# One gated-recurrence-and-mixer kernel: rows of 112 become rows of 96, two summands meet on TensorE, signs come from bits, and a new written-out order

## The chip, the cores and the metric

The kernel runs on one core of one Trainium2 chip. The metric is device microseconds from start to end of one execution. Before the change the median of 3 runs is 630.09 us (629.67 to 630.41). The profile is that of one execution. The engines are named as the profile names them: PE is TensorE's matrix multiplication and PEld its loading of weights, DVE is VectorE, ACT is ScalarE, POOL is GpSimd, and SP is SyncE, which issues most of the transfers.

## The reference

Two blocks follow each other. The first is a linear recurrence with a complex gate, for 4 batches, 8 heads, 768 steps and 48 elements a head:

```
mag = sqrt(a_re^2 + a_im^2);  scale = min(mag, 0.999) / (mag + 1e-6)
for t:  S = (a_re + i a_im)[t] * scale[t] * S + k[t] v[t]^T      (the imaginary part of k v^T is 0)
        y[t] = q[t] . Re S
```

The second is a mixer over the joined heads (384 columns). It mixes the steps with a product of rank 32, and then applies two layers with 1,536 hidden columns:

```
u = x + ((x^T U) V)^T
out = u + max(u W1, 0) W2
```

## The kernel before, in words

**Tiling.** A chunk is 128 steps of one batch with all heads, so there are 24 chunks, six to a batch. Two chunks are a group (12 groups). The mixer works on two chunks at a time (12 mixers, numbered 0 to 11), and a batch's three mixers can start only when its six chunks have run, since the rank-32 product sums over all steps. The tables of the weights arrive as 64-bit numbers and are turned into 32-bit ones on DVE and ACT in 13 pieces (`single`), all of it in the first 150 us.

**The gates of a group** (`magnitudes_of`, `within`, `of_blocks`, `turns_of`, `angles`). From `a_re` and `a_im` ACT and DVE form two things: the logarithm of the clipped magnitude, held in `l` after a second summand `y` has been added to it, and the angle, held in `z`. PE then multiplies the logarithms by constant matrices: `mid` gives tile `es ps`, `fore` gives tile `ef ps`, and `total` gives tile `tot`. ACT takes exponentials of these. The angles go through the matrix `prefix` into `ph`. The sign of `a_re` is needed in the angle. For groups 0 to 2 (`BITS`) DVE takes it from the sign bit; from group 3 on ACT computes it with Sign, and one ACT Identity later scales and shifts the angle. From group 3 on (`SPLIT`) the operands of these products are two fp32r parts each (`GS`): ACT (`MADE`) or DVE makes the first part and DVE the remainder.

**A chunk** (`prep`, `chain`). `q` and `k` are multiplied by the exponentials, then by cosine and sine into `QKC`. There a head holds 64 columns of real parts (48 used, 16 zeros) and after them 48 of imaginary parts, so that 112 columns of a head become 112 partitions when PE transposes it (tile `tr`, L860). ACT copies the result into `QK`. Products within the chunk follow (`inner` at L910 and L907, `corners`), DVE scales `QK` in between, a masked copy goes to `DG` and by DMA to `AT`, and `dk` and `y` are the products for the state and the output (L996, L1027, L1035).

**The mixer** (`mixer`). `rank` sums over a batch, `mixed` spreads it, `uTp` transposes, `up` (L1122) is the first layer, and `down` (L1313 for mixer 0, L1356 for the others) is the second. Mixer 0 starts its first layer before batch 0's rank product is known. It is put right afterwards (`put_right`): `rT` (L1136), `rw ps` (L1145), and six `fix` tiles (L1161), which are added to the hidden columns before `down` may use them.

**What sets the order.** Every operation is recorded with its engine. The table `ORDER` gives each one its place in one common row, numbered from 0 to 2670, and each engine executes its own operations in that order. `SPARE` says ahead of which places PE gets filler products of the identity with itself, in blocks of 128 columns, up to three blocks to a product (L1519). A filler is written into a PSUM tile that is free at that place, and is left out where none is free. PE, ACT, DVE, POOL and SP thus each wait in order: an instruction that waits holds up all that stand behind it on its engine.

The two lines that cut the widths, and the call that issues a filler:

```
    DP = 64
    DQ = DP + D
...
        nc.tensor.matmul(out=to[:, 0:k * 128].rearrange("p (k m) -> p k m", k=k), lhsT=ident,
                         rhs=ident.unsqueeze(1).to_broadcast([128, k, 128]), start=True, stop=True)
```

Of the kernel before, what the change touches and what calls it, by code (L numbers as in the profile page):

```python
# [39 lines left out]
        ("POOL", "load"): {0: [14], 1: [34], 1.5: [84], 2: [31]},  # L40
        ("DVE", "load"): {1: [58]},
# [6 lines left out]
        ("ACT", "gates"): {0: [1, 2, 4, 6, 7, 16, 17, 22, 23, 29, 28, 45, 70, 71], 1: [24, 27, 38, 39, 41, 42, 46, 47, 65, 64, 67, 68], 2: [129, 108,  # L48
# [10 lines left out]
        ("DVE", "gates"): {0: [5, 8, 13, 18, 19, 54, 49], 1: [30, 21, 40, 43, 44, 51, 50], 2: [111, 143, 156, 185, 169], 4: [277, 322, 323, 372, 356],  # L59
# [109 lines left out]
        ("POOL", "small"): {0: [932, 933], 1: [1119, 1116, 1117], 2: [1337, 1278, 1338], 3: [1670, 1446, 1515], 4: [1778, 1776, 1777], 5: [2049, 1855,  # L169
        2008], 6: [2154, 2101, 2162], 7: [2343, 2276, 2342], 8: [2633, 2632, 2648], 9: [2629, 2634, 2663], 10: [2635, 2627, 2636]},  # L170
        ("POOL", "angles"): {6: [615], 8: [708, 733], 10: [882, 931], 12: [1097], 14: [1273, 1302], 16: [1472, 1516], 18: [1669], 20: [1879, 1913],
        22: [2039, 2077]},
        ("DVE", "mixing"): {7: [2018, 2019, 2021, 2030, 2032, 2024, 2040, 2102, 2108, 2115, 2120, 2125, 2027]},
}

# [1413 lines left out]
```

## Time and profile before

| what | before |
|---|---|
| median of 3 runs | 630.09 us |
| span of the profiled execution, first to last instruction | 627.0 us |
| PE busy in it | 609.9 us (97%) |
| DVE busy | 499.7 us (80%) |
| ACT busy | 415.8 us (66%) |
| POOL busy | 38.1 us (6%) |
| moved by DMA | 45.74 MB, mean 73 GB/s |

The span is that of one execution and lies 3.1 us under the median of the timed runs. Busy time of PE counts every product, the fillers too. The page cuts the span in 40 slices of 15.7 us and gives busy tenths of each engine. A table by windows gives the same for stretches of one's own choice, with the clock that TensorE was granted. A row of the timeline gives a start, a duration, the engine, the line, the tiles and the number of merged records; in brackets stands the idle time before it and what ended it. Most fp32 products show as two records, a transpose as one.

### The profile page before, as it was taken

How to read it: one execution, taken by the hardware profiler on the slowest of the kernel's cores; microseconds unless marked ns; L12 is line 12 of the kernel's file. 1: busy time of each engine (PE TensorE's matmuls, PEld its weight loads, DVE VectorE, ACT ScalarE, POOL GpSimd, SP SyncE). 2: the span in 40 equal slices, each digit the busy share in tenths (PEclk: the TensorE clock that was granted, in tenths of full speed). 3: DMA queues.
4: the chain of work that ended last, by engine and by line, in shares of the span. 5: the costliest groups of instructions: out<-in, count | busy, mean ns of one | idle time of the engine just before them, and what ended most of it. 6: DMA issues, size and time to landing. Idle time of an engine off the chain costs nothing.

```text
span 627.0 us, 23447 instructions
## 1 busy us (share of the span) xinstructions
PE 609.9 (97%) x10380; PEld 526.2 (84%) x10380; DVE 499.7 (80%) x887; ACT 415.8 (66%) x807; POOL 38.1 (6%) x79
## 2 busy tenths in 40 slices
PE   6998989999999999999999999999999999999998
PEld 3566767666889889889989989888999998999997
DVE  6899999888999979758977867788989884464554
ACT  6999999999898988687787867688433431202010
POOL 5000000000001010010000100000100100000100
PEclk7999999999999999999999999999999999999999
DMA  8864565644143252541512512601203020000101
GB/s 211 191 146 115 135 136 132 155 111 104 33 80 76 50 120 44 99 89 28 99 37 46 113 40 46 124 19 25 63 21 60 9 51 3 1 1 1 45 14 44
DMA packets 173685, 45.74 MB, mean 73 GB/s; under 512 B 167632, under 2 KB 170384, under 8 KB 173584
## 3 DMA queue, kind: packets, MB, share of 16 engines
q1 hardware_dynamic: 171376, 39.90, 30.1%
q0 software_dynamic: 2208, 4.35, 2.1%
q8 instruction: 81, 1.33, 0.9%
q14 instruction: 20, 0.16, 0.1%
HBM read 33.59 MB, written 4.72 MB: 61 GB/s over the span
## 4 chain that ended last, share of the span: by engine, by line
PE 77%; ACT 4%; DVE 3%; DMA 1%; issue 1%; SPq 0%; ACTq 0%; DVEq 0%
PE down L1356 24%; PE up L1122 15%; PE few L1222 11%; PE dk L996 3%; PE tr L860 3%; PE y L1035 3%; PE inner L910 2%; PE down L1313 2%; PE inner L907 2%; PE tot L741 2%; PE y L1027 2%; PE mixed L1089 2%; PE es ps L692 1%; PE ef ps L692 1%; PE uTp L1107 1%; PE corners L971 1%
## 5 line engine op out<-in xcount | busy, mean ns | idle before, releaser
L1122 PE MATMUL up<-uT,w 128*128 128x256 f32 x504 | 116.9, 383 | 0.0
L387 DVE TENSOR_TENSOR QK<-QK,T 112x512 f32<-112x512 f32 (+2 forms) x144 | 102.1, 732 | 8.4 <-PE inner L910 4.3
L1122 PEld LDWEIGHTS up<-uT,w 128*128 128x128 f32 x504 | 93.6, 190 | 12.5
L1356 PE MATMUL down<-w,h 128*128 128x192 f32 x396 | 72.2, 331 | 0.0
L384 ACT ACTIVATE gate<-gate 128x768 f32<-128x768 f32 (+1 forms) x82 | 64.8, 795 | 7.4 <-DVE GS L791 3.2
L1356 PEld LDWEIGHTS down<-w,h 128*128 128x128 f32 x396 | 64.1, 190 | 1.5 <-issue 0.7
L871 ACT COPY QK<-tr 112x512 f32<-112x512 f32 x96 | 51.2, 590 | 14.6 <-PE tr L860 14.3
L390 DVE TENSOR_TENSOR xo<-down,xo 128x192 f32<-128x192 f32 (+1 forms) x79 | 29.9, 387 | 27.5 <-PE down L1356 27.0
L387 DVE TENSOR_TENSOR QKC<-qk,cs 128x768 f32<-128x768 f32 x44 | 41.7, 955 | 6.3 <-ACT cs L384 3.6
L1230 ACT COPY h<-few 128x512 f32<-128x512 f32 x30 | 17.2, 586 | 40.8 <-PE few L1222 40.8
L1356 PE MATMUL down<-stage 128*128 128x192 f32 x198 | 37.6, 331 | 0.0
L1111 ACT COPY uT<-uTp 128x384 f32<-128x384 f32 x22 | 10.0, 479 | 41.4 <-PE uTp L1107 26.9
L1222 PE MATMUL few<-gate,w 128*128 128x128 f32 x280 | 34.8, 275 | 0.0
L1298 POOL DMA_DIRECT2D out_dram<-xo x32 | 19.2, 644 | 243.3 <-DVE xo L390 140.0
L860 PEld LDWEIGHTS tr<-ident,QKC 64*112 64x112 f32 x768 | 24.5, 130 | 10.7 <-issue 4.7
L1222 PEld LDWEIGHTS few<-gate,w 128*128 128x128 f32 x280 | 33.3, 192 | 0.0
L1356 PEld LDWEIGHTS down<-stage 128*128 128x128 f32 x198 | 32.1, 190 | 0.7 <-issue 0.2
L779 POOL DMA_DIRECT2D gate<-F x15 | 12.0, 799 | 327.9 <-DVE w L578 113.5
L860 PE MATMUL tr<-ident,QKC 64*112 64x64 f32 x768 | 29.4, 221 | 2.3 <-DVE QKC L387 1.6
L381 ACT ACT_TABLE_LOAD x24 | 30.8, 1283 | 1.1 <-PEq L1573 0.7
L384 ACT ACTIVATE h<-up 128x512 f32<-128x512 f32 x42 | 24.6, 596 | 9.8 <-PE up L1122 9.5
L976 ACT COPY AT<-corners 32x128 f32<-32x128 f32 x96 | 24.2, 255 | 9.6 <-PE corners L971 8.3
(200 smaller groups left out, 1285.4 us busy)
## 6 DMA issues: line engine op xcount, KB each, us to landing
stage<-in_moe_w_ch_dram SPq DMA_DIRECT2D x12, 768.0 KB, 5.0
qk<-in_q_dram SPq DMA_DIRECT2D x24, 192.0 KB, 3.2
qk<-in_k_dram SPq DMA_DIRECT2D x24, 192.0 KB, 2.7
VP<-in_v_dram SPq DMA_DIRECT2D x24, 192.0 KB, 3.6
gate<-in_a_re_dram SPq DMA_DIRECT2D x22, 192.0 KB, 3.4
gate<-in_a_im_dram SPq DMA_DIRECT2D x22, 192.0 KB, 3.4
AT<-DG SPq DMA_DIRECT2D x96, 32.0 KB, 2.3
T<-E SPq DMA_DIRECT2D x48, 48.0 KB, 2.9
```

The costliest lines, as they stand in the source:

```text
L381: ACT(1.37, rank, lambda: nc.scalar.preload_act_table_set(name), writes=[TABLE])
L384: return nc.scalar.activation(out=o, in_=i, func=f, **kw)
L387: nc.vector.tensor_tensor(out=o, in0=a, in1=b, op=OP.mult)
L390: nc.vector.tensor_tensor(out=o, in0=a, in1=b, op=OP.add)
L860: nc.tensor.transpose(out=get(*ps[r])[0:DQ, h], in_=get(*qkc)[at, h].rearrange("p u d -> p (u d)")[:, 0:DQ], identity=ident[at, at], tile_ ...
L871: nc.scalar.copy(out=to, in_=a)
L976: ACT(0.36, RR, lambda r=r, u=u: nc.scalar.copy(out=get(*ATi).rearrange("p (a u) t -> p a u t", u=2)[r:r + BLK, :, u, BLK:2 * BLK], in_=ge ...
L996: nc.tensor.matmul(out=get(*dk[r])[x:end, h], lhsT=get(*ks)[at, h, x // DP, 0:end - x], rhs=get(*VPi)[at, h], start=True, stop=True, tile_ ...
L1122: nc.tensor.matmul(out=get(*ps)[:, e], lhsT=w1[:, f, (ff + e) * 128:(ff + e + 1) * 128], rhs=get(*uT)[:, f], start=(f == 0), stop=(f == KD ...
L1222: nc.tensor.matmul(out=get(*ps)[:, q], lhsT=w()[:, q * 128:(q + 1) * 128], rhs=v[0](), start=(n == 0 and q == 0), stop=True, skip_group_ch ...
L1298: queue.dma_start(out=out[b, c * CH:(c + 1) * CH, lo:hi], in_=get("xo", i)[:, lo:hi])
L1356: nc.tensor.matmul(out=get(*to)[:, part], lhsT=x(j), rhs=y[:, j], start=(first and j == 0), stop=(j == KH - 1), skip_group_check=not first)
```

## The change

1. The imaginary parts follow the real parts of a head at column 48 instead of 64: `DQ` is 96 instead of 112. `QKC` loses its zero columns between the parts, its multiplications write 768 columns in a row, and the transposes have 96 columns. The two products for the state still write partitions 0 to 63 and 64 to 111, the last 16 of them from the next head's columns, and only 96 are read. The 112 partitions of the tables `T` become 96, and the three memsets of `T` go.
2. In group 0 alone (`SUMMED`) DVE no longer adds `y` to `l`. Each product of the logarithms is done twice instead, once with `y` and once with `l`, accumulated in PSUM.
3. The sign of `a_re` comes from its bits on DVE in all groups. The ACT Sign of groups 3 to 11 goes, and so does their ACT Identity. The shift by a quarter moves into the two operations that make the fp32r parts.
4. `ORDER` and `SPARE` are replaced: another order on every engine and the transfer queues, 2,660 places instead of 2,671, and fillers at other places. 91 filler blocks are issued before (its table asks for 153, and the rest find no free tile) and 89 after, all that its table asks for. After, 24 of them stand ahead of the very first product of the program, where before there were 8.

The diff, cut:

```
-    DQ = DP + D
+    DQ = 2 * D
...
+    SUMMED = (0,)
...
-        QKC.append(singles.tile([128, H, 2, DP], FP, name="QKC%d" % n))
-        nc.gpsimd.memset(QKC[n][:, :, :, D:DP], 0.0)
+        QKC.append(singles.tile([128, H * DQ + DP - (DQ - DP)], FP, name="QKC%d" % n))
+        nc.gpsimd.memset(QKC[n][:, H * DQ:], 0.0)
...
         TS.append(singles.tile([DQ, GC, H * NTOT], FP, name="T%d" % n))
-        nc.gpsimd.memset(TS[n], 1.0)
...
-            if on_dve:
+            if g in SUMMED or g in SPREAD:
                 DVE(c_one(W), R1, lambda: nc.vector.tensor_scalar(out=t(l), in0=t(l), scalar1=-0.5, scalar2=-LNMAX, op0=OP.mult,
                                                                   op1=OP.max), [], [L])
-                DVE(cd, R1, lambda: add(t(l), t(l), t(y)), Y, [L])
+                if g not in SUMMED:
+                    DVE(cd, R1, lambda: add(t(l), t(l), t(y)), Y, [L])
...
-            if g in BITS:
-                DVE(c_one(W), R1, lambda: nc.vector.tensor_scalar(out=t(n).bitcast(U32), in0=t(ar).bitcast(U32), scalar1=0x80000000,
-                                                                  scalar2=INV_PI, op0=OP.bitwise_and, op1=OP.bitwise_or), AR, [N])
-            else:
-                ACT(ca + 0.09, R1, lambda: act(t(n), t(ar), AF.Sign, bias=tiny), AR, [N])
+            DVE(c_one(W), R1, lambda: nc.vector.tensor_scalar(out=t(n).bitcast(U32), in0=t(ar).bitcast(U32), scalar1=0x80000000,
+                                                              scalar2=INV_PI, op0=OP.bitwise_and, op1=OP.bitwise_or), AR, [N])
...
-                    PE(0.65, R1, lambda: nc.tensor.matmul(out=get(*to), lhsT=m.bitcast(FP), rhs=of(l, i), start=True, stop=True),
-                       [L, name], [to, ("sums", g, i)], takes=[keeps], steps=2)
+                    def each():
+                        for u, a in enumerate(parts):
+                            nc.tensor.matmul(out=get(*to), lhsT=m.bitcast(FP), rhs=of(a, i), start=(u == 0), stop=(u == len(parts) - 1))
...
-            if g not in BITS:
-                ACT(ca + 0.09, R2, lambda: act(t(z), t(z), AF.Identity, scale=1.0 / math.pi, bias=fourth), [], Z)
...
-                    ACT(c_act(DM), R2, lambda: nc.scalar.copy(out=of(a, i), in_=of(z, i)), [zi], [a + (i,)])
+                    ACT(c_act(DM) + 0.09, R2, lambda: act(of(a, i), of(z, i), AF.Identity, bias=fourth), [zi], [a + (i,)])
...
-                DVE(c_dve(DM), R2, lambda: nc.vector.tensor_tensor(out=of(b, i), in0=of(z, i), in1=of(a, i).bitcast(FP), op=OP.subtract),
-                    [zi, a + (i,)], [b + (i,)])
+                DVE(c_dve(DM), R2, lambda: nc.vector.scalar_tensor_tensor(out=of(b, i), in0=of(z, i), scalar=0.25, in1=of(a, i).bitcast(FP),
+                                                                          op0=OP.add, op1=OP.subtract), [zi, a + (i,)], [b + (i,)])
```

The two tables of `SPARE`, which read "place: filler blocks ahead of it":

```
-SPARE = {20: 8, 32: 9, 62: 1, 66: 1, 73: 1, 82: 5, 91: 1, 113: 6, 116: 1, 119: 8, 140: 8, 153: 6, 157: 4, 167: 1, 168: 1, 207: 6, 216: 1, 217: 1, 282:
-         1, 352: 2, 436: 1, 514: 5, 518: 5, 527: 4, 546: 4, 547: 25, 551: 12, 596: 2, 601: 1, 606: 3, 624: 1, 632: 3, 646: 1, 653: 1, 664: 1, 672: 2,
-         678: 5, 694: 1, 695: 1, 717: 1, 718: 2}
+SPARE = {28: 24, 79: 6, 86: 2, 100: 9, 118: 4, 143: 9, 151: 3, 158: 2, 193: 2, 217: 3, 237: 1, 257: 5, 262: 2, 270: 4, 287: 1, 294: 4, 301: 1, 311: 1,
+         519: 3, 587: 1, 606: 2}
```

More of the change, by code (lines that the diff above doesn't have):

```diff
@@ L30 @@
 ORDER = {
[9 rows of a table removed]
-        ("POOL", "load"): {0: [14], 1: [34], 1.5: [84], 2: [31]},
-        ("DVE", "load"): {1: [58]},
[6 rows of a table removed]
-        ("ACT", "gates"): {0: [1, 2, 4, 6, 7, 16, 17, 22, 23, 29, 28, 45, 70, 71], 1: [24, 27, 38, 39, 41, 42, 46, 47, 65, 64, 67, 68], 2: [129, 108,
[10 rows of a table removed]
-        ("DVE", "gates"): {0: [5, 8, 13, 18, 19, 54, 49], 1: [30, 21, 40, 43, 44, 51, 50], 2: [111, 143, 156, 185, 169], 4: [277, 322, 323, 372, 356],
[10 rows of a table removed]
-        ("ACT", "angles"): {0: [72, 86, 98, 100, 103], 1: [76, 106, 112, 114, 126], 2: [210, 231, 251, 240, 241, 242, 263, 269, 271], 4: [375, 395,
[5 rows of a table removed]
@@ L172 @@
[L172 to L178 removed]
[9 rows of a table added]
+        ('POOL', 'load'): {0: [11], 1: [62], 1.5: [586], 2: [34]},
@@ new lines @@
+        ('DVE', 'load'): {1: [29]},
[6 rows of a table added]
+        ('ACT', 'gates'): {0: [0, 3, 5, 12, 17, 13, 19, 39, 45, 33, 32, 41, 66, 67], 1: [9, 15, 23, 26, 25, 27, 43, 54, 53, 51, 60, 64], 2: [123, 61,
[10 rows of a table added]
+        ('DVE', 'gates'): {0: [6, 2, 21, 18, 68, 49], 1: [16, 8, 36, 30, 58, 46], 2: [94, 147, 154, 205, 210], 4: [265, 290, 303, 344, 299], 6: [401,
[10 rows of a table added]
+        ('ACT', 'angles'): {0: [71, 85, 91, 92, 98], 1: [80, 95, 107, 116, 112], 2: [211, 225, 239, 238, 232, 243, 251, 250, 256], 4: [369, 385, 413,
[5 rows of a table added]
+        ('DVE', 'angles'): {0: [74, 88], 1: [82, 96], 2: [216, 231, 241], 4: [377, 394, 417], 6: [567, 573, 577, 589, 616, 618, 631], 8: [703, 721,
[4 rows of a table added]
@@ new lines @@
+        ('DVE', 'prep'): {0: [78, 99, 101], 1: [110, 117, 128], 2: [223, 246, 253], 3: [236, 258, 310], 4: [348, 418, 419], 5: [402, 441, 491], 6:
[6 rows of a table added]
+        ('ACT', 'prep'): {0: [120, 115, 121, 119], 1: [137, 159, 160, 161], 2: [260, 277, 274, 272], 3: [291, 305, 328, 335], 4: [434, 439, 440, 438],
[4 rows of a table added]
+        ('DVE', 'rest'): {0: [111, 153, 155, 170, 146, 157, 173], 1: [175, 213, 219, 234, 222, 249, 255, 263], 2: [278, 318, 331, 379, 292, 334, 365,
[8 rows of a table added]
+        ('DVE', 'levels'): {0: [122, 133, 142, 132, 134, 150], 1: [164, 182, 188, 177, 186, 229], 2: [289, 295, 297, 296, 298, 314], 3: [337, 350,
[9 rows of a table added]
@@ new lines @@
+        ('ACT', 'levels'): {0: [140], 1: [201], 2: [304], 3: [393], 4: [477], 5: [538], 6: [747], 7: [808], 8: [942], 9: [1023], 10: [1169], 11:
[14 rows of a table added]
+        ('ACT', 'rest'): {0: [192, 184, 178, 190, 228, 230, 214], 1: [245, 252, 244, 254, 288, 283, 285], 2: [357, 362, 376, 370, 400, 399, 410], 3:
[10 rows of a table added]
+        ('ACT', 'small'): {0: [605, 307, 375, 447, 381, 523, 534, 611, 620, 626], 1: [738, 777, 798, 796, 809, 822, 769], 2: [882, 916, 1081, 1103,
[4 rows of a table added]
+        ('DVE', 'small'): {0: [316, 607, 635, 641, 642, 656, 664, 676, 643, 646, 754, 725], 1: [712, 729, 713, 830, 813, 821, 851, 900, 893, 904, 905,
[25 rows of a table added]
@@ L301 @@
     PL = H * HC
-    BITS = range(SPLIT[0])
     PUT = (0, 2), (4, 6), (8, 10)
@@ L734, in sums @@
                         h, w = at + (u * HH + p) * D, 64 if u == 0 else D
-                        nc.tensor.matmul(out=get(*ps)[u * 64:u * 64 + w, p], lhsT=get(*l)[:, h:h + w], rhs=total, start=True,
-                                         stop=True, tile_position=(0, u * 64))
+                        for n, a in enumerate(parts):
+                            nc.tensor.matmul(out=get(*ps)[u * 64:u * 64 + w, p], lhsT=get(*a)[:, h:h + w], rhs=total, start=(n == 0),
+                                             stop=(n == len(parts) - 1), tile_position=(0, u * 64))
             def at_once():
@@ L744, in of_blocks @@
             else:
-                PE(0.51, R1, sums, [l, ("total", 0), ("sums", g)], [ps], way=1, takes=[e], steps=4 * HH)
+                PE(0.2 + 0.31 * len(parts), R1, sums, [l, ("total", 0), ("sums", g)] + [y + (i,)] * (g in SUMMED), [ps], way=1, takes=[e],
+                   steps=4 * HH * len(parts))
             used = 2 * D if g in SPLIT else 64 + D
@@ L994, in state @@
                     at = slice(r * HC, (r + 1) * HC)
-                    for x, end in ((0, DP), (DP, DQ)):
-                        nc.tensor.matmul(out=get(*dk[r])[x:end, h], lhsT=get(*ks)[at, h, x // DP, 0:end - x], rhs=get(*VPi)[at, h],
+                    for x, w in ((0, DP), (DP, D)):
+                        nc.tensor.matmul(out=get(*dk[r])[x:x + w, h], lhsT=get(*ks)[at, h * DQ + x:h * DQ + x + w], rhs=get(*VPi)[at, h],
                                          start=True, stop=True, tile_position=(r * HC, x))
```

41 lines of the change are left out of this document (19 added, 22 removed), and 248 rows, old and new, of the table ORDER.

## The prediction

> **What bounds the kernel now.** I read the page first: busy times, then the slices.
>
> ```profile
> PE 609.9 (97%) x10380; PEld 526.2 (84%) x10380; DVE 499.7 (80%) x887; ACT 415.8 (66%) x807; POOL 38.1 (6%) x79
> ...
> PE   6998989999999999999999999999999999999998
> ```
>
> PE is busy throughout, but part of that is filler. So I asked for windows, first of everything, then of the filler line L1519 alone (columns: window, length, then busy us of PE, PEld and the rest).
>
> ```profile
> 0.00:30.00 30.00, 23.25 (x118) 13.62 (x118) 23.08 (x50) 22.91 (x45) 8.41 (x32) 0.89 0.84 203
> 30.00:62.00 32.00, 30.07 (x819) 21.50 (x820) 31.66 (x52) 31.07 (x60) 0.00 (x0) 1.00 0.58 134
> 62.00:98.00 36.00, 32.30 (x860) 24.59 (x856) 35.10 (x56) 35.27 (x67) 0.00 (x0) 1.00 0.54 126
> 98.00:126.00 28.00, 27.61 (x491) 19.88 (x487) 25.86 (x42) 26.03 (x51) 0.96 (x1) 1.00 0.61 150
> 126.00:157.00 31.00, 30.08 (x290) 19.76 (x290) 27.34 (x39) 28.45 (x46) 1.53 (x2) 1.00 0.47 109
> 157.00:627.00 470.00, 466.58 (x7830) 426.82 (x7822) 356.66 (x653) 272.12 (x542) 27.16 (x44) 1.00 0.24 49
> ```
>
> ```profile
> 0.00:30.00 30.00, 14.16 (x36) 8.30 (x36) 0.89 0.84 203
> 30.00:62.00 32.00, 8.65 (x30) 4.83 (x28) 1.00 0.58 134
> 62.00:98.00 36.00, 1.08 (x4) 0.68 (x4) 1.00 0.54 126
> 98.00:126.00 28.00, 2.59 (x8) 1.19 (x8) 1.00 0.61 150
> 126.00:157.00 31.00, 4.12 (x16) 2.71 (x16) 1.00 0.47 109
> 157.00:627.00 470.00, 0.00 (x0) 0.00 (x0) 1.00 0.24 49
> sum 627.00, PE 30.61 PEld 17.70; mean PE 5.10 PEld 2.95
> ```
>
> Two stages are to be seen. After 157 us PE runs no filler and is idle for 470.0 - 466.6 = 3.4 us, nearly all of it behind the last product: this stage lasts as long as its products. Before 157 us DVE and ACT are the full engines (66.76 and 66.34 of 68 us from 30 to 98), and PE lacks operands: it is idle for 157.0 - 143.3 = 13.7 us and turns filler for 30.6. I call both together lost time: 44.3 us to 157, 47.7 in all, beside 579.3 us of the kernel's own products. The span is own products plus lost time, and I forecast the two separately. The span of 627.0 lies 3.1 us under the median of 630.09; I carry this difference over.
>
> **The milestone.** The rows that I use from the timeline (start, duration, engine, line, records):
>
> ```profile
> 1.42 3.58 PE L1519 MATMUL tr<-ident 128*128 128x384 f32 x6 [1.42 <-POOL ident masks.py:199]
> 8.79 1.62 PE L696 MATMUL es ps<-GL,mid 128*128 128x384 f32 x2 [3.79 <-DVE GL L390]
> 10.21 4.05 PE L1519 MATMUL tr<-ident 128*128 128x384 f32 x6
> ...
> 16.00 0.81 PE L696 MATMUL ef ps<-GL,fore 128*128 128x384 f32 x2
> ...
> 107.22 0.70 PE L907 MATMUL inner<-QK 112*16 112x16 f32 x64
> ...
> 125.99 1.16 PE L1161 MATMUL fix<-V,rw 32*128 32x256 f32 x16
> ...
> 157.01 5.45 PE L1122 MATMUL up<-uT,w 128*128 128x256 f32 x24
> ```
>
> At 157.01 mixer 1 starts its first layer. I followed, in each kernel's listing of the instructions in order, which ACT and DVE instructions stand at or ahead of the last one that this product waits for, and added the mean busy time of their forms in this trace. Before: 263 on ACT, 144.8 us, and 221 operations on DVE behind the memsets, 141.1 us. Changed: 257 on ACT, 139.6, and 218 on DVE, 138.8. The products ahead of it on PE are worth the same in both lists, but for the doubled ones of group 0.
>
> **The change part by part.**
>
> ```profile
> L860 PE MATMUL tr<-ident,QKC 64*112 64x64 f32 x768 | 29.4, 221 | 2.3 <-DVE QKC L387 1.6 <-DVE F L807 0.6
> L860 PEld LDWEIGHTS tr<-ident,QKC 64*112 64x112 f32 x768 | 24.5, 130 | 10.7 <-issue 4.7 <-DVE QKC L387 2.5 <-DVE F L807 1.0
> L1107 PEld LDWEIGHTS uTp<-ident,xo 128*128 128x128 f32 x72 | 9.0, 141 | 1.0 <-issue 0.4
> L387 DVE TENSOR_TENSOR QKC<-qk,cs 128x768 f32<-128x768 f32 x44 | 41.7, 955 | 6.3 <-ACT cs L384 3.6 <-PE tr L860 1.6 <-PE dk L996 0.9
> L387 DVE TENSOR_TENSOR qk<-qk,es 128x768 f32<-128x768 f32 x22 | 20.9, 953 | 1.4 <-DMA qk<-in_q_dram 1.4
> ```
>
> *Rows of 96.* The moving 64 columns of a transpose stay; its weights shrink by 16 columns of 112. Bounds: nothing, or one seventh of the 29.4 us, 4.2. The two loads for transposes above (130 ns with 112 columns, 141 with 128) say 0.7 ns a column, so 11 ns of each load, and two loads run side by side in the halves of the array: 768 x 11 / 2 = 4.2 again, if the load alone sets the pace. I take half, 2.1 us, because the stream of the identity is as long as before. 34 of the 48 sets of 16 stand behind the milestone, so 1.5 us come off the span; those ahead of it only enlarge a wait. The Trainium skill, TensorE: Matmul & The Clock Gate, section LDWEIGHTS, says that the time of a load goes by its columns; by its figure the 768 loads would shed some 5 us between two halves, an estimate, and the sum would then be about 2 us lower than mine. DVE gains nothing from writing 768 in a row: the strided write above takes 955 ns, the plain one 953. Products for the state, masks and transfers keep their sizes. The memsets of `T` delay nothing:
>
> ```profile
> 1.82 1.45 POOL L469 MEMSET T<- 112x512 f32 x3
> 5.43 0.70 POOL L484 TENSOR_TENSOR mid<-prefix 128x128 fp32r<-128x128 f32 x1 [2.16 <-DMA prefix<-in_spans_dram]
> ```
>
> POOL then waits 2.16 us for a transfer.
>
> *Group 0.* Four products of 384 columns more, 0.81 each by the row at 16.00, and the totals twice: 3.7 to 4.3 us on PE by the rows here and below; I take 3.7 (they overlap in the stream). DVE sheds 2 x 0.57.
>
> ```profile
> L735 PE MATMUL tot<-total,GL 128*64 128x32 f32 x32 | 2.2, 223 | 0.7 <-ACT es L384 0.7
> L390 DVE TENSOR_TENSOR GL<-GL,gate 128x384 f32<-128x384 f32 x2 | 1.1, 568 | 0.3 <-ACT gate L384 0.2
> L384 ACT ACTIVATE gate<-gate,tiny 128x768 f32<-128x768 f32 x9 | 8.4, 938 | 0.0
> L384 ACT ACTIVATE gate<-gate,fourth 128x768 f32<-128x768 f32 x9 | 8.4, 931 | 2.3 <-DVE gate L760 2.1
> L578 DVE TENSOR_SCALAR w<-w 128x768 uint32<-128x768 uint32 x12 | 6.7, 562 | 0.0
> ACT gate L384 <- PE ef ps L696: 2.0, 1, 2.0
> ```
>
> The cover is the 14.2 us of filler before 30 us. Without that cover the 3.7 us would go onto the span whole.
>
> *Signs from bits.* ACT loses 8.4 + 8.4 us and gains about 16 x 0.1 for the shift, so 15.2 net. DVE gains 9 x 0.562 = 5.1. Behind 157 us both are hidden: DVE is busy 356.7 of 470 us there. Ahead of it only groups 3 and 4 count, and they are in the totals of the milestone.
>
> *The order.* It decides which totals stand ahead of what. ACT's is 5.2 us smaller at the milestone, DVE's 2.3. DVE ends last with the smaller gain, so I let the milestone come 2.3 us earlier. The bounds are 0 (a wait on PE, not work, sets it) and 5.2. Of the transfers on SP's queue, the gate rows of the second chunk and the masks, 480 KB, now go ahead of the first piece of a weight table: at the 203 GB/s of the first window this piece lands up to 2.4 us later. DVE meets it behind nine operations of group 0 and waits for little; I put it at 0, with 2.4 as the bound. 89 filler blocks against 91 change nothing by their number, but behind the first 67 us or so the new order has only six, so PE has no room there.
>
> **The sum.** Own products: 579.3 + 3.7 - 1.5 = 581.5. Lost time: 44.3 - 2.3 - 3.7 = 38.3 to the milestone (the doubled products take the place of filler), 3.4 behind it. Together 623.2, that is 3.8 under the span of before, and 626.3 as a median.
>
> **The rivals.**
>
> *Larger gain: the start too.* Before, PE stands idle for 3.79 us, and its next products run at half pace: three fillers in 4.05 us, 1.35 each, against 0.81 at 16.00; ACT waits 2.0 us for `ef ps`. Changed, eight fillers stand in front. If three take until 5.0 as before and five more 0.65 each, they end at 8.2, close to the first real product, and these run at full pace. Then 2.0 us more come off, and 3.0 for the transposes (34 of 48 of 4.2): 627.0 - 2.3 - 2.0 - 3.0 = 619.7, a median of 622.8. The rule in the skill's page TensorE: Matmul & The Clock Gate, section Part 1, that an idle window of about 3.4 us halves the clock and a busy one restores it, speaks for this case; by it the trace agrees with the idle 3.79 us. Against it: DVE may wait for loads instead.
>
> *No change.* The front fillers run at half pace throughout: they end at 1.42 + 8 x 1.28 = 11.7, and the eight sums of group 0 after them at 1.35 each end later than the 16.8 of before, by about 2.8 if the sums start at 8.8 at best. That eats the 2.3: 626.0, a median of 629.1.
>
> *Slower: the stretch from chunk 5 to the first `fix`.* L907 of chunk 5 starts at 107.22 with 98.6 us of ACT work and 94.7 of DVE work ahead; changed it has 101.8 and 98.9, so it starts by up to 4.2 us later, at 111.4. From there `y`, `rank`, `rT`, `rw` and `fix` follow one another, 18.8 us to 125.99. With the same 18.8 the first `fix` comes at 130.2. The listing puts 90.0 us of own products ahead of it (86.7 by the windows, and 3.3 more), so 40.2 are lost, and the sum is 581.5 + 40.2 + 3.4 = 625.1. Should the chain lengthen by the waits that it has already (ACT and DVE idle for 4.5 and 5.8 us from 98 to 157; say 5.1), because PE no longer has filler there that can give way, the span is 630.2 and the median 633.3. It is slower by more than 0.2% once the first `fix` comes after 133.4.
>
> **How the numbers follow.** The forecast has 0.45, the larger gain 0.17, no change 0.13, the slower case 0.25. The predicted time is 626.3, from the likeliest. Its own range is 623.4 (ACT's 5.2 instead of 2.3) to 628.2 (the chain of 18.8 us). The runs shown spread by 0.1%, so about 0.2%, 1.3 us, is what can be told from no change. Faster: 0.45 + 0.17 = 0.62; same 0.13; slower 0.25. The range runs from 620.5, a little under the larger gain, to 632.5, within the slower case; it leaves out the upper part of that case.
>
> **What would show it.** Right: no filler row and no wait of PE behind 130 us; L860 at about 28 us or less in all; the product of mixer 1's first layer about 155 us; ACT about 14 us less busy, DVE about 4 more. Wrong: the first `fix` after 133 us; waits of PE on ACT or DVE between 65 and 130 us that sum to more than 5 us; half pace of the sums of group 0; L860 unchanged.

## The result and the profile after

The changed kernel takes 636.54 us (median of 4 runs, 631.11 to 638.93) against 629.88 us for the kernel before on the same chip (628.22 to 630.41). The ratio is 1.0107, with a 95% interval of 1.0073 to 1.0141: slower by about 1%. The forecast was 626.3 us, and 623.2 us for the span of the profiled execution; that span is now 633.5 us (time 635.32 us). The chips differ a little, so every kernel below was timed beside the kernel before (628.0 to 628.4 us in those series), and its ratio counts.

The page of the kernel after (busy times, then two rows of the 40 slices):

```profile
PE 617.6 (97%) x10402; PEld 530.3 (84%) x10402; DVE 500.8 (79%) x893; ACT 402.1 (63%) x789; POOL 35.2 (6%) x76
...
PE   9999799899999999999999999999999999999998
...
PEclk9999899899999999999999999999999999999999
```

ACT shed 13.7 us, about as forecast. PE is busier by 7.7 us. The last row is the granted clock: it dips in the fifth and the eighth slice. Three windows of the prediction, taken again (columns as there), and then two windows cut at the milestone, first for everything and then for the filler line, now L1521:

```profile
62.00:98.00 36.00, 32.23 (x653) 24.68 (x655) 29.66 (x49) 29.59 (x56) 0.00 (x0) 0.91 0.59 140
98.00:126.00 28.00, 25.99 (x682) 20.90 (x670) 25.25 (x43) 23.81 (x50) 0.08 (x1) 0.94 0.58 124
...
157.00:633.50 476.50, 470.36 (x7955) 429.57 (x7953) 363.42 (x666) 266.27 (x537) 28.15 (x45) 1.00 0.25 50
```

```profile
0.00:159.56 159.56, 149.84 (x2580) 102.97 (x2581) 139.92 (x232) 138.26 (x257) 7.08 (x31) 0.97 0.59 137
159.56:633.50 473.94, 467.80 (x7823) 427.37 (x7822) 360.86 (x662) 263.84 (x532) 28.15 (x45) 1.00 0.25 50
...
0.00:159.56 159.56, 26.88 (x74) 14.19 (x74) 0.97 0.59 137
159.56:633.50 473.94, 0.00 (x0) 0.00 (x0) 1.00 0.25 50
```

From 62 to 98 us DVE and ACT, full before (35.1 and 35.3 us), are idle for 6.3 and 6.4 us, PE for 3.8, and the clock is 0.91. So in this stretch all three wait for something else. Behind 157 us PE is idle for 6.1 us where it was 3.4. PE's own waits, the longest first (the columns: what waited, on what, us in all, times, longest), and the place of the first in the timeline of PE:

```profile
PE tot L734 <- issue: 3.6, 1, 3.6
PE y L1029 <- DMA AT<-DG: 3.1, 3, 1.4
```

```profile
73.40 0.42 PE L734 MATMUL tot<-total,GL 128*64 128x32 f32 x8
77.42 0.53 PE L734 MATMUL tot<-total,GL 128*64 128x32 f32 x8 [3.60 <-issue]
77.88 4.93 PE L1124 MATMUL up<-uT,w 128*128 128x256 f32 x12
...
114.57 0.67 PE L1029 MATMUL y<-VP,AT 64*64 64x48 f32 x28 [1.03 <-DMA AT<-DG]
...
116.23 4.53 PE L1124 MATMUL up<-uT,w 128*128 128x256 f32 x12
...
159.56 2.78 PE L1124 MATMUL up<-uT,w 128*128 128x256 f32 x12
```

Between two like groups of products of one operation PE stops for 3.60 us, and "issue" says that nothing in the profile held it. The next `up` runs at half pace, 4.93 us where others take 2.8 to 2.9. A second half-paced `up` follows a wait for a transfer. The last row is the milestone, mixer 1's first product: 159.56 us, against 157.01 before and 154.7 forecast. The kernel before has one wait of the same kind, at 96.84 us, which stood in the list of its waits before the prediction was made:

```profile
PE inner L907 <- issue: 1.0, 1, 1.0
```

What stops PE can be seen in the transfers. Queues of the kind "instruction" bring the engines their instructions. This is the row of q8, the larger of the two, for the whole execution; then come the queues of two windows ahead of 77.42 us:

```profile
q8 instruction: 82, 1.34, 0.9%
```

```profile
DMA packets 2602, 1.07 MB, mean 219 GB/s; under 512 B 2387, under 2 KB 2387, under 8 KB 2602
...
q1 hardware_dynamic: 2602, 1.07, 95.5%
...
stage<-in_moe_w_ch_dram SPq DMA_DIRECT2D x1, 768.0 KB
gate<-in_a_im_dram SPq DMA_DIRECT2D x2, 192.0 KB, 5.3
...
q1 hardware_dynamic: 984, 0.29, 108.9%
q8 instruction: 1, 0.02, 5.3%
```

82 packets of 16 KB go with 2 x 10,402 records of PE and PEld (81 with 2 x 10,380 in the kernel before). I take q8 to be PE's queue, so that one packet holds about 254 of its instructions, an estimate that runs 1 and 6 bear out. In a window this short a queue's share can come out above 100%. From 70.0 to 74.9 us none moves (the first four rows), while data keep the DMA engines 95.5% busy: a 768-KB piece of w2 (issued at 71.15 us) and 192-KB loads. From 74.9 to 76.0 us one moves (the last two), and PE goes on at 77.42. That the wait is a late packet was so far a reading; the experiments test it.

### The profile page after: what moved, and what is told of

It reads as the page before. It is cut to its first block, busy times and chain, and to the rows that moved or that the text cites. A ratio compares the mean times of both kernels' runs of the same rounds, so it can differ in the third digit from the quotient of the medians.

```text
span 633.5 us, 23493 instructions
## 1 busy us (share of the span) xinstructions
PE 617.6 (97%) x10402; PEld 530.3 (84%) x10402; DVE 500.8 (79%) x893; ACT 402.1 (63%) x789; POOL 35.2 (6%) x76
## 4 chain that ended last, share of the span: by engine, by line
PE 74%; ACT 8%; issue 6%; DVE 4%; SPq 3%; DMA 3%; POOL 0%; ACTq 0%; DVEq 0%; POOLq 0%
PE down L1358 21%; PE up L1124 15%; PE few L1224 11%; PE dk L998 3%; PE y L1037 3%; PE tr L862 3%; PE down L1315 3%; PE inner L912 2%; ACT gate L383 2%; DMA AT<-DG 2%; PE y L1029 2%; PE mixed L1091 2%; PE tot L740 2%; PE inner L909 1%; PE uTp L1109 1%
## 5 line engine op out<-in xcount | busy, mean ns | idle before, releaser
L1124 PE MATMUL up<-uT,w 128*128 128x256 f32 x504 | 120.4, 392 | 0.0
L386 DVE TENSOR_TENSOR QK<-QK,T 96x512 f32<-96x512 f32 (+2 forms) x144 | 102.4, 725 | 11.0 <-PE inner L912 6.1
L1124 PEld LDWEIGHTS up<-uT,w 128*128 128x128 f32 x504 | 96.3, 195 | 14.3 <-ACT h L383 0.6
L873 ACT COPY QK<-tr 96x512 f32<-96x512 f32 x96 | 51.0, 586 | 12.3 <-PE tr L862 12.2
L862 PEld LDWEIGHTS tr<-ident,QKC 64*96 64x96 f32 x768 | 24.4, 123 | 9.8 <-DVE QKC L386 4.5
L862 PE MATMUL tr<-ident,QKC 64*96 64x64 f32 x768 | 29.8, 220 | 0.8 <-DVE QKC L386 0.6
L998 PEld LDWEIGHTS dk<-VP,QKC 64*64 64x64 f32 (+1 forms) x1408 | 25.0, 127 | 4.2 <-issue 1.2
```

The source lines that it names most:

```text
L386: nc.vector.tensor_tensor(out=o, in0=a, in1=b, op=OP.mult)
L862: nc.tensor.transpose(out=get(*ps[r])[0:DQ, h], in_=get(*qkc)[at, h * DQ:(h + 1) * DQ], identity=ident[at, at], tile_position=(r * HC, 0))
L873: nc.scalar.copy(out=to, in_=a)
L998: nc.tensor.matmul(out=get(*dk[r])[x:x + w, h], lhsT=get(*ks)[at, h * DQ + x:h * DQ + x + w], rhs=get(*VPi)[at, h], start=True, stop=True, ...
L1124: nc.tensor.matmul(out=get(*ps)[:, e], lhsT=w1[:, f, (ff + e) * 128:(ff + e + 1) * 128], rhs=get(*uT)[:, f], start=(f == 0), stop=(f == KD ...
```

## The experiments

Theory: PE runs out of instructions where a packet is late, half clock follows, and this carries the loss before the milestone; transfers from DG to AT behind 192-KB loads on SP's queue carry the rest. Rivals: the 20 doubled products of group 0 are on the path; the rows of 96 or the signs on DVE cost the time. The table gives every profiled execution, split at mixer 1's first `up` product (us from its timeline; "behind" is the span less the milestone).

| kernel | median us | ratio to before (95%) | milestone | behind it |
|---|---|---|---|---|
| before (first profile) | 630.09 | 1 | 157.0 | 470.0 |
| forecast | 626.3 | | 154.7 | 468.5 |
| after | 636.54 | 1.0107 (1.0073 to 1.0141) | 159.6 | 473.9 |
| 1 e1_phase | 633.60 | 1.0084 (1.0059 to 1.0108) | 158.4 | 473.0 |
| 2 e2_load_later | 634.17 | 1.0096 (1.0064 to 1.0128) | 161.9 | 472.5 |
| 3 e4_added_on_dve | 635.55 | 1.0136 (1.0064 to 1.0208) | 158.4 | 472.1 |
| 4 e5_order_before | 633.51 | 1.0077 (1.0054 to 1.0101) | 158.1 | 475.4 |
| 5 e6_load_behind | 631.10 | 1.0038 (1.0018 to 1.0059) | 155.0 | 473.7 |
| 6 e7_phase_worst | 636.57 | 1.0146 (1.0096 to 1.0195) | 164.5 | 476.0 |
| 7 e8_places_first | 638.29 | 1.0166 (1.0129 to 1.0202) | 160.8 | 475.7 |
| 8 e9_two_parts | 628.81 | 1.0008 (0.9996 to 1.0019) | 156.5 | 471.0 |
| 9 e10_two_places | 628.32 | 1.0003 (0.9987 to 1.0019) | 154.9 | 470.5 |
| 10 e11_two_places_phase | 630.49 | 1.0038 (1.0022 to 1.0054) | 156.1 | 473.3 |
| 11 e12_load_behind_added | 630.54 | 1.0049 (1.0021 to 1.0077) | 155.7 | 472.1 |
| 12 e13_more_places | 628.30 | 1.0007 (0.9989 to 1.0025) | 155.6 | 470.8 |

In kernels with an edited order the table takes 113 lines less: L621 there is L734, L749 L862, L885 L998, L916 L1029, L1011 L1124.

### 1. Other starts of the packets

```diff
         while run:
-            idle(min(run, AHEAD))
-            run -= min(run, AHEAD)
+            k = 1 if at < 40 else min(run, AHEAD)
+            idle(k)
+            run -= k
```

> The kernel after, with one edit: the 24 filler blocks at its start are issued as 24 products of one block in place of 8 products of three. The tensor engine does the same work in the same order, with 16 more products in its instruction stream ahead of everything else, so each packet of instructions ends earlier in the work than before. Theory (the tensor engine ran out of instructions: the packet that begins with the totals' product at 77.42 us in the kernel after came late, 3.60 us, and half clock followed): the product at 77.42 us no longer stands at the start of a packet, its 3.60 us go, and with them the half clock behind it; 636.5 - 3.9 - 2.1 = 630.5 us, unless another packet comes late at its new place. Rival (that product waits for something of the order itself, or the doubled products, the rows of 96 or the signs on VectorE cost the time): nothing of these is touched, 636.5 us, and the wait stands where it stood.

It took 633.6 us. The stop at the totals' product at 77 us is gone, but others came. PE's timeline, and windows between its stops (the first two counts are PE's and PEld's records):

```profile
67.02 0.49 PE L1109 MATMUL uTp<-ident,xo 128*128 128x128 f32 x3 [2.09 <-ACT w L383]
...
89.32 0.24 PE L998 MATMUL dk<-VP,QKC 64*48 64x48 f32 x2 [1.30 <-issue]
...
106.44 0.87 PE L740 MATMUL tot<-total,GL 128*96 128x32 f32 x9 [1.09 <-issue]
```

```profile
67.02:89.30 22.28, 20.92 (x381) 15.19 (x381) 19.54 (x31) 18.65 (x37) 0.00 (x0) 0.92 0.64 156
89.32:106.43 17.11, 15.77 (x381) 13.32 (x381) 15.84 (x26) 14.93 (x27) 0.00 (x0) 1.00 0.35 84
```

Both windows hold 762 instructions of PE, three packets of 254. So the stops stand at the starts of packets, also the first, which the profile puts down to ACT. With the same work and 16 more products at its head, the kernel stops elsewhere: the theory was right on the place and wrong on the gain of 6 us, since PE meets other late packets. Here too SP's queue issues a 768-KB piece of w2 in front of each: at 59.63, 83.20 and 99.38 us, and the packets move at 64.0, 87.0 and 104.0 us or up to 0.5 us later.

### 2. The 768-KB load later, its conversions too

```diff
-('SP', 'load')  7.1: [364]            ('ACT', 'w2') 0: [384, 420]      ('DVE', 'w2') 0: [409, 431, 456]
+('SP', 'load')  7.1: [404.5]          ('ACT', 'w2') 0: [437.5, 441.5]  ('DVE', 'w2') 0: [442.5, 447.5, 456]
```

> The kernel after, with the 768-KB load of w2's first part (issued at 71.15 us on SP's queue in the kernel after) moved behind the two loads of a_im, of q and k and the first totals' transfer, to about 79.5 us, and the five conversions of it on ScalarE and VectorE moved behind its new landing. Theory (that load, with the others at 70 to 76 us, held up the packet of instructions): the packet lands sooner by about the load's own 2.7 us or more, the wait of 3.60 us falls under 1 us, no half clock follows, 630 to 632 us. Rival (packets do not queue behind data, or the wait is not for a packet): the wait stays at 3.6 us and the time at 636.5 us.

634.17 us. The stop fell to 1.1 us as the theory has it, but the time hardly moved: at 95.29 us `inner` waits 2.68 us for DVE, which the moved conversions hold up, and half clock follows that. The edit had a price of its own; run 5 takes it away.

### 3. Group 0's logarithms added on DVE again

```diff
-    SUMMED = (0,)
+    SUMMED = ()
-('DVE', 'gates') 0: [6, 2, 21, 18, 68, 49]         1: [16, 8, 36, 30, 58, 46]
+('DVE', 'gates') 0: [6, 2, 21, 18, 27.5, 68, 49]   1: [16, 8, 36, 30, 46.5, 58, 46]
...
-            idle(min(run, AHEAD))
-            run -= min(run, AHEAD)
+            k = 1 if at < 82 else min(run, AHEAD)
+            idle(k)
+            run -= k
```

> The kernel after, with group 0's two logarithms added on VectorE again (one addition a chunk, in front of the multiplication by a_im) and its 20 doubled products taken out of TensorE's stream; the first two runs of filler are issued in single blocks (20 more products), so that the packets of instructions from 31 us on begin with the same products as in the kernel after. Theory (a late packet and its half clock carry the loss): the wait at about 77 us stays, and the time is 635 to 637 us; the doubled products took filler's place. Rival (the doubled products are on the path): 3.6 us less, 633 us.

635.55 us, and the stop stayed, though smaller (1.96 us, at the same product, 77.52 us) and without half clock behind it: the next `up` took 2.86 us. The interval, 1.0064 to 1.0208, holds the rival's 633 too: this run does not decide.

### 4. All parts, in the order of the kernel before

The edit is the whole table of places: that of the kernel before, with the signs' places on ACT given to DVE.

> The kernel after in all its parts (rows of 96, group 0's logarithms added on TensorE, signs from bits with the bias in the splitting), but in the order and with the filler of the kernel before: the signs stand on VectorE at the places that they had on ScalarE, and the places of what is gone are left out. Theory (the order carries the loss): about the kernel before, 629 to 631 us. Rival (the parts themselves cost the time): 634 to 637 us.

633.51 us: the theory that the new order alone carries the loss fell. The parts cost about 5 us in the old order too. PE's timeline:

```profile
396.01 1.24 PE L1245 MATMUL down<-stage 128*128 128x192 f32 x6
399.06 1.22 PE L916 MATMUL y<-VP,AT 64*64 64x48 f32 x32 [1.81 <-DMA AT<-DG]
400.21 1.09 PE L924 MATMUL y<-G,QK 96*64 96x48 f32 x16
401.10 1.06 PE L924 MATMUL y<-GM,QK 96*64 96x48 f32 x16
402.09 1.09 PE L749 MATMUL tr<-ident,QKC 64*96 64x64 f32 x16
```

The transfer for `y` is late by 1.81 us, and the products behind it run at half pace (0.64 to 0.67 us is usual for these sets of 16). Run 8 asks which part does it.

### 5. The 768-KB load alone moved, by three transfers

```diff
-('SP', 'load') 7.1: [364]     8.7: [354, 390]
+('SP', 'load') 7.1: [383.5]   8.7: [354, 383.4]
```

> The kernel after, with one change on SP's queue: the 768-KB load of w2's first part (issued at 71.15 us) moved behind the two a_im loads and the load of k that follow it, with all else, the conversions of that load too, where they were (ScalarE takes them up at 82.6 us in a run without the long wait). In the run with the load still later the wait at the totals' product fell from 3.6 to 1.1 us, but the moved conversions held up VectorE, 2.7 us at 94 us. Theory (a late packet of instructions and the half clock behind it carry most of the loss before mixer 1): the wait at about 75 us is 1 us or less, no half clock between 70 and 100 us, and the time is 630 to 633 us. Rival (the conversions, not the packet): no change, 635 to 637 us.

631.1 us, 5.4 us less than after by the medians (4.3 by the ratios), for one DMA issued some 3.6 us later. PE's timeline and SP's:

```profile
74.72 0.37 PE L621 MATMUL tot<-total,GL 128*64 128x32 f32 x8 [1.40 <-issue]
75.02 2.86 PE L1011 MATMUL up<-uT,w 128*128 128x256 f32 x12
```

```profile
72.64 1.20 SPq L417 DMA_DIRECT2D gate<-in_a_im_dram  x2
74.28 0.37 SPq L424 DMA_DIRECT2D qk<-in_k_dram  x1
74.77 0.51 SPq L445 DMA_DIRECT2D stage<-in_moe_w_ch_dram  x1
```

The stop is 1.40 us, `up` runs at full pace, and the milestone is at 154.95 us, 4.6 us earlier than after and 0.3 from the forecast. (I had expected at most 1 us of a stop.) The two intervals of the ratio lie apart, so the gain is clear of the noise.

How long the stop lasts is less clear. Two other kernels whose 768-KB load stands in front as in the kernel after, runs 3 and 7, show these rows in their profiled executions:

```profile
77.52 0.42 PE L621 MATMUL tot<-total,GL 128*64 128x32 f32 x8 [1.96 <-issue]
...
75.03 0.54 PE L621 MATMUL tot<-total,GL 128*64 128x32 f32 x8 [1.68 <-issue]
```

So 3.60 us is the size of one execution, and these two are only 0.3 to 0.6 us above the 1.40 us without the load. And 1.40 us remain although no data were in the way: this is the only queue row of run 5 from 72.0 to 73.2 us, and PE goes on at 74.72.

```profile
q8 instruction: 1, 0.02, 6.7%
```

### 6. The starts of the packets where PE is fastest

```diff
-            idle(min(run, AHEAD))
-            run -= min(run, AHEAD)
+            k = 1 if at < 105 else min(run, AHEAD)
+            idle(k)
+            run -= k
```

> The kernel after, with the first runs of filler (24, 6, 2 and 9 blocks, all before 27 us) issued in single blocks: 27 more products in the stream and the same work. By the starts of the run with the first 24 blocks single, the 256 instructions of a packet then last only 3.6 us at 64 us, 3.1 us at 85 us and 2.4 us at 100 us, where a packet took 1.0 to 2.2 us from the boundary to its start, 1.0 to 1.4 us to land and 1.4 us to the first instruction. Theory (TensorE is bound by its packets wherever 256 instructions last less than about 4 to 5 us): TensorE's waits of no named cause or right at a packet's start sum to 4 to 8 us between 60 and 110 us, at those places, and the time is 635 to 641 us. Rival (packets matter only where a large load stands in front): as with 24 single blocks, 632 to 634 us.

636.57 us. PE's timeline and the windows between:

```profile
69.42 0.33 PE L909 MATMUL inner<-QK 96*16 96x16 f32 x21 [2.44 <-issue]
...
92.19 0.56 PE L998 MATMUL dk<-VP,QKC 64*64 64x48 f32 x24 [1.82 <-issue]
...
109.75 0.44 PE L998 MATMUL dk<-VP,QKC 64*64 64x48 f32 x15 [2.16 <-issue]
```

```profile
69.40:92.10 22.70, 20.88 (x380) 15.14 (x381) 19.88 (x32) 18.56 (x37) 0.00 (x0) 0.92 0.64 154
92.19:109.70 17.51, 15.13 (x381) 12.66 (x381) 14.24 (x22) 14.75 (x27) 0.00 (x0) 1.00 0.33 79
```

Stops of 6.4 us in all, again three packets apart (761 and 762), some 5 to 10 us later than I had placed them. With equal work, only the cuts between packets differ from run 1, and the time differs by 3 us (1.0084 against 1.0146; the intervals overlap by a little).

The rival on large loads is not excluded by this run. SP's queue issues 768-KB pieces of w2 at 61.87, 85.91 and 102.58 us, and the packets of the three stops move within 66.5 to 67.0, 89.5 to 90.0 and 107.0 to 107.5 us, so each stands some 4 to 5 us behind such a load. Other starts bring other packets behind these loads; only what is left of the stop in run 5, 1.40 us, stands without one.

### 7. The four transfers of a chunk at once

Each chunk from the seventh on has its four places made consecutive, for example:

```diff
-('SP', 'place') 7: [862, 910, 877, 886]
+('SP', 'place') 7: [862, 862.1, 862.2, 862.3]
```

> The kernel after, with the four transfers from DG to AT of each chunk from the seventh on issued one right behind the other on SP's queue (at the place of the first of the four), so that no 192-KB load stands between them. In the kernel after y's first product waited for the last of the four at 114.6, 196.9, 263.9 and 398 us, 1.0, 1.4, 1.0 and 0.8 us in its trace. Theory (the order puts loads between them): the waits after 130 us go, lost time after mixer 1's first product falls from 3.8 to about 1 us, the time to 633 to 634 us beside an unchanged early stretch. Rival (the transfers are late because the chip's queues are full, or because DG is): no change, or the pushed loads are late in their place and gates wait for them.

638.29 us, more than the theory had, and the sign that the rival named is there. No wait of `y` for DG to AT behind 130 us was left, but a load that was pushed back was late in its turn (waits of ACT and PE from 250 to 330 us):

```profile
ACT gate L270 <- DMA gate<-in_a_re_dram: 3.5, 1, 3.5
...
PE uTp L996 <- DVE F L693: 1.4, 1, 1.4
```

The early stretch was not unchanged, though: besides the stop of 1.68 us shown above there was one of 2.10 us at 102.93 us with half pace behind it, and the milestone came 1.2 us later than after. The intervals of this run and of the kernel after overlap, so what the pushed loads cost is not shown.

### 8. Two parts in the old order: rows of 96 and signs from bits

The edit is run 4's with `SUMMED = ()` and the two additions at their old places.

> The kernel before in its order and with its filler, with two of the parts alone: rows of 96, and the signs from bits with the bias in the splitting; group 0's logarithms are added on VectorE as before, and TensorE's stream has as many products as before. With all three parts in that order the time was 633.5 us against 628.4. Theory (in that order the 20 doubled products push TensorE 2 us later than its transfers were timed for, and the late DG to AT transfer at 397 us with half clock follows from that): about the kernel before, 627 to 630 us. Rival (the rows of 96, or the signs on VectorE, cost the time): 632 to 634 us.

628.81 us, 1.0008: in that order these two parts cost nothing and gain nothing. Run 4 differs from it by the doubled products alone, so in that order they cost 4.7 us (633.51 - 628.81): 1.7 ahead of the milestone and 4.3 behind it in the profiled executions, the latter at the late transfer of run 4. Here the transposes read:

```profile
L749 PE MATMUL tr<-ident,QKC 64*96 64x64 f32 x768 | 29.2, 220 | 2.3 <-DVE QKC L273 1.6 <-DVE F L693 0.7
...
L749 PEld LDWEIGHTS tr<-ident,QKC 64*96 64x96 f32 x768 | 24.0, 123 | 10.7 <-issue 4.7 <-DVE QKC L273 2.5 <-DVE F L693 1.1
```

### 9. Run 5, and two transfers put forward

```diff
-('SP', 'place') 7: [862, 910, 877, 886]     16: [1795, 1813, 1778, 1791]
+('SP', 'place') 7: [862, 886.5, 877, 886]   16: [1795, 1795.5, 1778, 1791]
```

> The kernel with the 768-KB load behind (631.1 us, with waits of y for the transfers from DG to AT of 1.6 us at 192.5 us and 1.0 us at 393.2 us), and one more change on SP's queue: of chunk 7 and of chunk 16 the last of the four transfers is issued ahead of the one 192-KB load (chunk 7) and of the load, the totals' transfer and chunk 17's first transfer (chunk 16) that stood in front of it. Theory (these two waits are what is left of the loss): they fall under 0.3 us and the time to 628 to 629.5 us, that of the kernel before. Rival (with all the transfers from the seventh chunk on put first, the loads behind them were late, and it was 638 us; so one wait is exchanged for another): 630.5 to 632 us.

628.32 us, ratio 1.0003: the time of the kernel before is back, by three transfers moved on SP's queue (the load of k only keeps its place ahead of the first). The intervals of runs 5 and 9 just touch. PE's waits:

```profile
PE tot L621 <- issue: 1.1, 1, 1.1
PE rw ps L1034 <- DVE rw L1027: 1.0, 1, 1.0
PE y L916 <- DMA AT<-DG: 0.8, 3, 0.3
```

### 10. Run 9 with the packets begun 20 instructions earlier

```diff
-            idle(min(run, AHEAD))
-            run -= min(run, AHEAD)
+            k = 1 if at < 40 and run > 17 else min(run, AHEAD)
+            idle(k)
+            run -= k
```

> The same as the kernel with two transfers put forward, with 5 more products in the first run of filler (24 blocks as 13 products in place of 8, the same work), so that the packets of TensorE's instructions begin 20 instructions earlier in the work. By the starts of the run with 24 single blocks, that is the phase with the fewest packets whose 256 instructions last under 5 us before 160 us. Theory (packets cost time wherever they are short): 0.5 to 1.5 us less than without the 5 products, 627 to 628.5 us. Rival (what is left of the packets' waits is not worth a microsecond): no difference.

630.49 us, 2 us more where I expected 1 less. The stop before `up` fell only from 1.1 to 0.9 us (at `corners`, 74.72 us), while at 110.91 us `y` waited 1.03 us for DG to AT and the next `up` took 4.54 us. Counting short packets is no way to choose a phase: it leaves out what else the shift moves.

### 11. Run 5 with group 0 added on DVE

```diff
-    SUMMED = (0,)
+    SUMMED = ()
-('DVE', 'gates') 0: [6, 2, 21, 18, 68, 49]         1: [16, 8, 36, 30, 58, 46]
+('DVE', 'gates') 0: [6, 2, 21, 18, 19.5, 68, 49]   1: [16, 8, 36, 30, 30.5, 58, 46]
...
-            idle(min(run, AHEAD))
-            run -= min(run, AHEAD)
+            k = 1 if at < 82 else min(run, AHEAD)
+            idle(k)
+            run -= k
```

> The kernel with the 768-KB load behind (631.1 us), with group 0's two logarithms added on VectorE again, each right after the logarithm that it needs, the 20 doubled products out of TensorE's stream and 20 more products of filler by single blocks, so that the packets begin with the same products from 31 us on. Up to 64 us the products behind the filler start 0.05 us after the VectorE instruction that they need: TensorE waits there for VectorE. Theory (in this order the doubled products cost nothing and the two additions, 0.55 us each, delay VectorE): 1 to 2 us slower than with the load behind alone, 632 to 633 us. Rival (the doubled products are on the path): up to 3.6 us faster, 627.5 us.

630.54 us, between the two expectations and not to be told from run 5 (1.0049 and 1.0038, intervals overlapping). In the new order the 20 doubled products neither cost nor gain anything that these runs could show.

### 12. Run 9 with three more moves

```diff
-('SP', 'load') 8.7: [354, 383.4]    ('SP', 'place') 4: [498, 497, 525, 505]     11: [1239, 1235, 1217, 1223]
+('SP', 'load') 8.7: [372.5, 383.4]  ('SP', 'place') 4: [498, 497, 519.5, 505]   11: [1223.7, 1223.4, 1217, 1223]
```

> The kernel with the 768-KB load behind and the transfers of chunks 7 and 16 put forward (628.3 us, the time of the kernel before), with three more moves on SP's queue of the same kind: chunk 5's load of k (at 68 us) moved behind chunk 2's transfers, to just before the a_im loads, the last transfer of chunk 4 put ahead of two loads of a_re and a_im (108 us), and two of chunk 11's ahead of a totals' transfer and of a load (254 us). Theory (TensorE still waits 1.1 us for a packet at 74 us, and 0.3 to 0.5 us each for chunk 4's, 5's and 11's transfers): 0.5 to 1.5 us less, 627 to 628 us, at or just under the kernel before. Rival (the moved loads are late in their place): 629 us or more.

628.3 us, no gain; PE's stop at the totals is still 1.1 us. No version that I ran beats the kernel before.

## Why the prediction was wrong

The profiled span missed its forecast by 10.3 us: 4.9 ahead of the milestone (159.6 for 154.7) and 5.4 behind it (473.9 for 468.5).

- **The order, ahead of the milestone: the step that failed.** I counted ACT's and DVE's work, let the milestone come 2.3 us earlier, and put the transfers at nothing after looking at the first window alone. What I left out is that PE's own instructions come by the same DMA engines; the 1.0 us of "issue" in the kernel before was a sign of it. In the profiled execution PE stopped for 3.60 us behind a 768-KB load, and half clock added 2.1 us to the next `up` (4.93 for 2.86). With that one load moved the stop was 1.40 us, half clock did not follow, and the milestone came at 154.95 us, 4.6 us earlier. The count itself fits: 154.7 forecast, 154.95 in run 5 and 154.86 in run 9. That it fits so closely is partly luck, since both executions still hold a stop, of 1.40 and 1.14 us, that the count does not have.
- **Own products and lost time.** The sum's two terms did not come out apart as I had them. In the kernel after, own products are 617.64 - 26.88 = 590.8 us (581.5 forecast) and lost time 42.7 (41.7): half pace makes products longer, so part of what the order cost stands under own products. In run 9 (busy 613.3 us, filler 26.5) the two are 586.8 and 38.6 us, one 5.3 us above the forecast and the other 3.1 below. Ahead of the milestone own products are 123.0 us after and 119.6 in run 9, for 116.4 forecast. In run 9 this error is made up by lost time, since PE has time there; why the products are longer is open.
- **The term behind the milestone, 3.4 us of lost time.** I carried it over from the kernel before, although the order rearranges SP's queue there too. It measured 473.9 - 467.8 = 6.1 us after, and 3.3 us in run 9. `y` waited for DG to AT at 196.86 us for 1.42 us, and for less at two later places; putting two transfers forward took the stage from 473.7 to 470.5 us. Putting all of them first removed the waits of `y` and made a load late.
- **Rows of 96: a term that was mis-sized.** 2.1 us were taken, 1.5 of them on the span; nothing was gained. The load fell from 130 to 123 ns, the way that the Trainium skill's page TensorE: Matmul & The Clock Gate, section LDWEIGHTS, has it, though by about half of the 13 ns that its figure gives for 16 columns, an estimate. But the products stayed at 220 ns (221 before), one of the signs that I had named for being wrong. Behind the milestone the transposes took 20.5 us after and in run 9 and 19.6 us in run 8, for 19.7 before. By that page's figure the sum would have gone further off. So the load did not set the pace.
- **Group 0.** 3.7 us in place of filler: nothing speaks against it in the new order (run 11 beside run 5). It is no general price, since in the old order the same products cost 4.7 us, most of it at one late transfer. Whether they make that transfer late by their time or by where the packets then begin is not told apart.
- **Signs from bits.** ACT shed 13.7 us for 15.2 forecast; DVE gained 1.1 us for 4.0. By its forms the sign operations added 4.9 us and the two additions took off 1.1, as forecast, and the rest came out about 2 us shorter in small amounts. Both are hidden, as run 8 confirms in the old order.
- **The rivals.** With the front fillers the first sums did run at full pace, as in the larger gain: the first starts at 9.44 us and takes 0.81, though the fillers end at 9.6 us and not at 8.2. But runs 5 and 9 reach the milestone no earlier than the plain forecast. The slower case had the right side for another reason: its condition, the first `fix` behind 133.4 us, was not met (132.31, and 127.30 in run 9), and the waits of PE on ACT or DVE between 65 and 130 us stayed small. No filler stood behind 130 us, as foretold, but waits did, and I had named no sign for a wait on instructions.

Put together, run 9 comes near the forecast by the profiled spans: 625.4 us against 623.2, and the transposes behind the milestone (20.5 us where 18.2 were forecast) make up the difference. By the ratio it does not. The forecast was 0.6% under the kernel before, and run 9 is level with it (1.0003); its profiled execution, 627.27 us, is one of its faster ones. So about 4 us of gain that I forecast did not come even with the transfers put right. The transposes explain 2.3 of them, an estimate from single executions, and the rest is open.

What stays open: why a packet takes its turn late at one place and not at another (with the load moved, 1.1 to 1.4 us of the stop remained, and with the load in front it was 3.60, 1.96 and 1.68 us), and why run 10 lost 2 us. Each placement of the late transfers was traced in one execution of its kernel.

## What to carry to other kernels

An engine with ten thousand short instructions is itself a user of the DMA queues: before costing a new order, look in the old kernel's trace for waits on instructions, and at which large load is issued ahead of each packet. A wait put down to "issue", or to an engine that was long done, that recurs at multiples of one packet's instructions is most likely such a stop, and moving one large load by three places can be worth most of a loss (here 4.3 of 6.7 us). An order of transfers belongs to one timing of the products: whoever shifts these by a microsecond or two must look at every transfer that lands just in time.

## What the runs showed of the hardware

- **Instructions can run out.** PE stopped for 1.1 to 2.4 us at places 761 to 762 of its records apart (runs 1 and 6), and for 3.60 us in the kernel after, where it resumed 1.4 us or more after the packet had moved. The Trainium skill, Runtime: NRT & Kernel Launch, section Instruction fetch mechanics, has blocks of 16 KB and 256 instructions, which the packets here agree with (16 KB, 254 records), and calls crossing a boundary "mostly hidden"; here it cost up to 3.60 us.
- **Half clock after short waits.** It followed waits of 3.60 us (4.93 for 2.86), 1.81 us (1.09 for 0.65) and 1.03 us (4.53 for 2.86), and did not follow others of 1.96 us (run 3), 1.42 us (196.86) and 1.40 us (run 5). The Trainium skill's page TensorE: Matmul & The Clock Gate, Part 1, asks for an idle window of about 3.4 us; the first case agrees, the short ones do not.
- **The clock column can miss half pace.** In run 8 `es ps` took 1.62 us at 8.72 us and the fillers behind it 4.05 us for six records, twice the usual, while the granted clock of the windows from 5 to 10 and from 10 to 15 us reads 1.00.
